# Fused attention and channel mix on one core: block 2 fetches its input tiles once for two mixes, and the parts of the kernel stand in a newly planned order

## The chip, the cores and the metric

The kernel runs on one core of a Trainium2 chip. The metric is the device time of one execution in microseconds (us), lower is better. The engines of the core are named as in the profile: PE (matmuls; PEld is its weight load), DVE (vector), ACT (scalar), POOL, and SP, whose queue issues nearly all DMA transfers.

## What is computed

An attention in two steps gives x, and a channel mix works on x. Sizes: 8 batches, 8 heads, 576 positions, head dimension 64, 32 pack keys; x has 8 x 576 = 4608 rows of 512; all inputs are fp32.

```
def attention(q, k, v, p):                  # per batch and head
    packed = softmax(p @ k.T / 8) @ v       # 32 x 64
    return softmax(q @ packed.T / 8) @ packed   # 576 x 64

x = heads side by side                      # (8, 576, 512)
x_prev = x one position later (zeros ahead of the first)
xk = mu_k * x + (1 - mu_k) * x_prev
xr = mu_r * x + (1 - mu_r) * x_prev
k = max(xk @ w_k, 0)                        # 512 -> 1024
v = (k * k) @ w_v                           # 1024 -> 512
out = sigmoid(xr @ w_r) * v
```

## The kernel before

**Blocks.** The 4608 rows of x are nine blocks of 512 rows (TB). Blocks 0, 1 and 2 are computed one by one: first `gates` (xr by w_r, 16 groups of matmuls), then `keys` (xk by w_k, 32 groups), then `values` (the squares by w_v, 32 groups). Blocks 3 and 4, 5 and 6, 7 and 8 are three pairs (PAIRS), in which products of sums of blocks and sums of weights are taken (`products_of`, L1499); the first pair's gates are `turned_gates` (L1655 to L1657, 32 groups). A product is split for precision: each operand is a high and a low part, and high by high, high by low and low by high are added. So a group is three matmuls of 128x128 by 512 columns, called a triple here (L1087 to L1089 and L1109 to L1111 in the gates, L1038 to L1040 in the keys, L1138 to L1140 in the values).

**Attention.** It runs batch by batch, its small matmuls set between the triples: `front` (L630, the pack queries by the 4 key tiles kT of a batch, 32 matmuls), L658 (the weights by v), L688 (a transpose), L786 (q by the packed keys; when it is done, the places of that batch's key and query tiles are free for a later batch's), and two groups of L835 (16 matmuls each), which make x of a batch. Batch 0, the first gates and the conversion of the weights into high and low parts (`convert`, L351 to L367) form the head of the program; where PE would have nothing to do there, it runs spare matmuls (L1833). The mixes of block 0 are made from PSUM in the head (`mixed_on_pe`: L892 on PE, L903 on ACT, L905 on DVE).

**The input of a block.** Blocks 0 and 1 (`FETCHED = 2`) take x from SBUF. From batch 1 on x is also stored in DRAM (the tiles xt into xd, 577 KB a store, one for two of the four 128-channel slices), and blocks from 2 on read it back. `mix(i, j, res, tag)` makes the four slices c of one mix of block i, one after another: it starts `fetch(i, c, j)`, waits for it, takes places, mixes (`mixed_parts`: L1006 on ACT times mu, then L1010 on DVE, which adds the shifted x) and starts `split` (L1019 on ACT: high part; L1021 on DVE: low part). It stands for xr and for xk of a block, so a slice is fetched twice. The places "xin" at block 2 are two.

**What sets the order.** Every part of the work is a generator with a rank. The class `Flow` holds the time at which each engine would be free by estimated durations, and at each step emits the instruction that could start first, the lower rank first where starts are equal. So the order of the instructions on PE, DVE, ACT and in SP's queue follows from the estimates and from a table of ranks at the top of the kernel; each engine then runs its own instructions strictly in that order on the chip, and SP issues its transfers in that order too, each when what it waits for has come. `load` (L247) is the estimate for a transfer: it takes one shared DMA resource for `us`, times 1.3 between 1.2 and 8 us, and `1.1 * us + 0.1` where it begins after 45 us.

**Squares.** `squared` takes a finished key group: ACT relu (L1050), ACT square (L1053), then the high part: on ACT (L1058) for the first `CASTS = 2` of the eight f of a block, on DVE (L1061) for the others; then the low part on DVE (L1063).

**Sums of weights.** For the pairs, DVE and ACT make sums of the split weights in spare time (`chain_of_sums`, tiles sw), which SP stores in DRAM (sum<-sw) and streams back later (ring<-sum).

Of the kernel before, what the change touches and what calls it, by code (L numbers as in the profile page):

```python
# [17 lines left out]
class Flow:  # L18
# [12 lines left out]
    HOLD = {}  # L31
    URGENT = 22.872
    CHANGE = 0.1
# [157 lines left out]
def attn_pack_channel_mix(ctx: ExitStack, tc: tile.TileContext, q, k, v, p, p_first, mu_first, mu_by_channel, w_k, w_v, w_r, out):  # L191
    nc = tc.nc
    B, NPR, P, S = q.shape
# [17 lines left out]
    flow = Flow()  # L211


    FIRST = 14.499, 7.547, 12.422, 11.979
    RANK_1, RANK_MIX, RANK_KEYS, RANK_R, RANK_W, RANK_W2, RANK_V, LOADS_1, RANK_SQ, RANK_REST, HOLD_V, HOLD_S = 12.717, 12.505, 15.753, 30, 30, 27.28, 30, 30, 0.73, -9.153, 0.319, 0.199
    RANK_LATE1 = -1.745
    RANK_LATE2 = 1.396
    RANK_LATE3 = 8.576
    RANK_LATE4 = 9.62
    RANK_LATE5 = 9.05  # L220
    RANK_LATE6 = 13.793
    RANK_LATE13 = 8.231
    RANK_LATE12 = -0.408
    FIRST_K, FIRST_V, FIRST_Q = (RANK_LATE1, RANK_LATE2), (RANK_LATE3, RANK_LATE4), (RANK_LATE5, RANK_LATE6)
# [20 lines left out]
    def load(dst, src, issue, us, queue="queue"):  # L245
        yield queue, issue, None, None
        dict(queue=nc.sync, scalar=nc.scalar, gpsimd=nc.gpsimd)[queue].dma_start(dst, src)  # L247
        begin = max(flow.free.get("dma", 0.0), flow.t + 0.46, SLOW[0])
        if begin < SLOW[1]:
            us *= SLOW[2]  # L250
        elif begin > 45.0:
            us = 1.1 * us + 0.1
        flow.free["dma"] = begin + us
        flow.free[queue] = max(flow.free[queue], begin - 2.0)
        flow.now.t = begin + us + LANDS

    LANDS = 2.0
# [5 lines left out]
    def reached():  # L263
# [12 lines left out]
    BUFS = dict(kq=7, vt=2, xin=0, pt=1, aT=4, pm=2, e=4, a2=1, xt=5, tmp=4, xk=NC, sq=NF, sig=4,  # L276
                pa=2, both=1, m=4, n=4, staged=4, ex=3, pair=0, ring=0, store=2, twin=0)
    for tag, n in BUFS.items():
# [9 lines left out]
    MORE = {("tmp", 4): "ex2"}  # L288
    RANK_B, RANK_TURN, RANK_BACK, RANK_OUT, RANK_L = 3.794, 1.444, 9.553, 2.981, 27.75
    CASTS = 2  # L290
    WHOLE = dict(wv=0)
    RANK_AHEAD = 9.346
    RANK_2, LOADS_2 = 11.443, 34.522
    RANK_SUMS = dict(k=26.146, v=2.238, r=29.743)
    CHAINS = dict(A=(13.692, 26.413), B=(37.551, 41.281), RB=(0.2, 15.996), C=(16.813, 2.931), RC=(3.842, 6.82))

# [655 lines left out]
    def mix(i, j, res, tag):  # L952

        yield from flow.wait("mu")
        rank = flow.now.rank
        for c in range(NC):
            if i < FETCHED:
                yield from flow.wait(*(("xt", b, c, hf) for b, *_ in pieces(i) for hf in range(2)))
            else:
                flow.spawn(fetch(i, c, j), rank)  # L960
                yield from flow.wait(("fetched", i, c, j))
            slot = yield from flow.take("xk" if tag == "xk" else "sq")
            space = "tmp"
            sx = yield from flow.take(space)
            x32 = tile_([P, TB], F32, space, sx, "x32")
            yield from (mixed if i < FETCHED else mixed_parts)(i, c, j, x32)
            flow.spawn(split(i, c, space, sx, x32, res, tag, slot), rank)
# [15 lines left out]

    fetched = {}

    def fetch(i, c, j):
# [3 lines left out]
        at, parts = 0, []  # L990
        for b, s, n, o in pieces(i):
# [4 lines left out]
            at += n + 1  # L996
        fetched[i, c, j] = slot, parts
        flow.set(("fetched", i, c, j))

    def mixed_parts(i, c, j, x32):  # L1000
# [7 lines left out]
        for n, o, x in parts:  # L1008
# [3 lines left out]
            )  # L1012
        flow.give("xin", slot)

# [734 lines left out]
    def channel_mix():  # L1749
# [16 lines left out]
        for i in PAIRS:  # L1766
# [4 lines left out]
            for t in range(NF // 2):  # L1771
                flow.spawn(operands_of_values(i, t), 1.091)
            for kind in KINDS[i]:
# [133 lines left out]
```

## Time and profile before

| | us |
|---|---|
| three runs | 552.84, 556.06, 553.84 |
| their median | 553.84 |
| the profiled execution, whole | 552.96 |
| its span in the profile | 551.2 |
| PE busy | 540.6 (98%) |
| DVE busy | 463.9 (84%) |
| ACT busy | 379.1 (69%) |

The span is the stretch from the first to the last instruction that the profiler recorded; the 1.8 us between it and the execution's own time lie around it. The profiled execution is 0.88 us below the median of the three runs. The granted clock of PE was 0.999 of full speed over the span.

### The profile page before, as it was taken

To read this page: it belongs to the slowest core of one execution; us is meant where nothing else is said; L and a number is where in the kernel's file an instruction comes from. 1 tells how busy PE (TensorE), PEld (TensorE's weight loads), DVE (VectorE), ACT (ScalarE), POOL (GpSimd) and SP (SyncE) were. 2 spreads that over 40 slices of the span, in tenths; PEclk is the share of its full clock that TensorE was granted. 3 is DMA by queue.
4 is the path that set the end of the run, shared out by engine and by line. 5 is a ranking of instruction groups with operands and counts; after the bars stand their busy time and mean duration, and the time that the engine had idled before them with its cause. 6 is when DMAs were issued, how large, how long until landed. Compare 5 with 4: busy or idle time off the path is not lost.

```text
span 551.2 us, 10089 instructions
## 1 busy us (share of the span) xinstructions
PE 540.6 (98%) x3541; PEld 416.6 (76%) x3541; DVE 463.9 (84%) x887; ACT 379.1 (69%) x730; POOL 2.8 (1%) x27
## 2 busy tenths in 40 slices
PE   8999999999999999999999999999999999999996
PEld 7857766766677777776887888887878888888885
DVE  2987989987799958898898999957999994799873
ACT  3789686556746756648899666589886648987650
POOL 1000000000000000000000000000000000000000
PEclk9999999999999999999999999999999999999999
DMA  8977967798977889697938537819273680924232
GB/s 301 401 282 242 398 225 262 234 296 266 298 245 238 273 284 347 194 319 237 318 135 278 199 134 226 252 50 294 78 229 95 219 259 28 303 92 153 76 134 96
DMA packets 90386, 123.89 MB, mean 225 GB/s; under 512 B 9824, under 2 KB 60512, under 8 KB 90336
## 3 DMA queue, kind: packets, MB, share of 16 engines
q1 hardware_dynamic: 89056, 121.87, 67.5%
q10 hardware_dynamic: 1280, 1.38, 0.7%
q8 instruction: 28, 0.46, 0.3%
q14 instruction: 22, 0.18, 0.1%
HBM read 89.38 MB, written 33.83 MB: 224 GB/s over the span
## 4 chain that ended last, share of the span: by engine, by line
PE 70%; DMA 14%; DVE 7%; ACT 5%; issue 2%; SPq 1%; POOL 0%; DVEq 0%; ACTq 0%; POOLq 0%
PE ph L1499 48%; DMA xin<-xd 3%; PE ph L1038 3%; PE ph L1039 2%; PE ph L1040 2%; DMA sum<-sw 2%; PE spare L1833 2%; DMA kT<-in_k 2%; DMA whole<-m 1%; PE pr L1656 1%; PE pr L1657 1%; PE pr L1655 1%; SPq L247 1%; PE pa L630 1%; DVE x L1010 1%
## 5 line engine op out<-in xcount | busy, mean ns | idle before, releaser
L1499 PE MATMUL ph<-vT,ring 128*128 128x512 f32 x270 | 66.5, 393 | 0.0
L1499 PEld LDWEIGHTS ph<-vT,ring 128*128 128x128 f32 x270 | 50.7, 188 | 11.5
L1499 PE MATMUL ph<-vB,wv_h 128*128 128x512 f32 x140 | 43.9, 395 | 0.1
L1499 PE MATMUL ph<-vT,wv_h 128*128 128x512 f32 x140 | 43.7, 394 | 0.0
L1138 PE MATMUL pvo<-wv_h,sq 128*128 128x512 f32 x96 | 39.5, 412 | 0.5 <-ACT r L1050 0.5
L1038 PE MATMUL ph<-xk,wk_h 128*128 128x512 f32 x96 | 39.2, 408 | 0.0
L1010 DVE SCALAR_TENSOR_TENSOR chain<-xin,mus,chain 128x320 f32<-128x320 f32 (+7 forms) x72 | 34.5, 509 | 5.1 <-ACT chain L1006 5.0
L1139 PE MATMUL pvo<-wv_l,sq 128*128 128x512 f32 x96 | 37.6, 391 | 0.0
L1039 PE MATMUL ph<-xk,wk_h 128*128 128x512 f32 x96 | 37.5, 391 | 0.0
L1040 PE MATMUL ph<-xk,wk_l 128*128 128x512 f32 x96 | 37.4, 390 | 0.0
L1140 PE MATMUL pvo<-wv_h,sq 128*128 128x512 f32 x96 | 37.4, 389 | 0.0
L1551 ACT COPY ph<-ph 128x512 f32<-128x512 f32 x44 | 25.4, 577 | 15.3 <-PE ph L1499 14.9
L1006 ACT ACTIVATE chain<-xin,mus 128x320 f32<-128x320 f32 (+7 forms) x72 | 35.3, 525 | 0.0
L1157 ACT CAST vT<-c 128x512 fp32r<-128x512 f32 x40 | 24.7, 619 | 14.7 <-PE ph L1499 12.8
L1163 DVE TENSOR_TENSOR c<-c 128x512 f32<-128x512 f32 x48 | 31.0, 685 | 0.0
L1499 PEld LDWEIGHTS ph<-vB,wv_h 128*128 128x128 f32 x140 | 26.1, 188 | 6.4 <-DMA wv_h<-sum 0.7
L1499 PEld LDWEIGHTS ph<-vT,wv_h 128*128 128x128 f32 x140 | 26.2, 188 | 6.0 <-ACT ph L1551 0.3
L1159 DVE TENSOR_TENSOR vT<-c,vT 128x512 fp32r<-128x512 f32 x40 | 26.7, 687 | 2.4 <-ACT vT L1157 2.3
L1499 PE MATMUL ph<-vB,wv_l 128*128 128x512 f32 x70 | 27.6, 395 | 0.3 <-DMA wv_l<-sum 0.3
L1499 PE MATMUL ph<-vT,wv_l 128*128 128x512 f32 x70 | 27.4, 391 | 0.0
L1163 DVE TENSOR_TENSOR chain<-chain 128x512 f32<-128x512 f32 x40 | 26.7, 685 | 0.3
L1159 DVE TENSOR_TENSOR vT<-chain,vT 128x512 fp32r<-128x512 f32 x32 | 21.4, 686 | 5.5 <-ACT vT L1157 5.3
(206 smaller groups left out, 1374.3 us busy)
## 6 DMA issues: line engine op xcount, KB each, us to landing
ring<-sum SPq DMA_DIRECT2D x56, 256.0 KB, 4.1
sum<-sw SPq DMA_DIRECT2D x40, 256.0 KB, 4.1
kT<-in_k SPq DMA_DIRECT2D x32, 288.0 KB, 5.5
qT<-in_q SPq DMA_DIRECT2D x32, 288.0 KB, 5.4
vt<-in_v SPq DMA_DIRECT2D x32, 256.0 KB, 4.7
out<-sig SPq DMA_DIRECT2D x32, 256.0 KB, 3.3
xd<-xt SPq DMA_DIRECT2D x14, 577.0 KB, 6.3
wv_h<-sum SPq DMA_DIRECT2D x28, 256.0 KB, 4.2
```

Source lines behind the costliest of these rows:

```text
L1006: nc.scalar.mul(x32[:, o:o + n], x[:, 1:], mus[:, j, c:c + 1])
L1010: nc.vector.scalar_tensor_tensor(x32[:, o:o + n], x[:, :n], mus[:, j + 1, c:c + 1], x32[:, o:o + n], op0=ALU.mult, op1=ALU.add,)
L1038: nc.tensor.matmul(ph, wk_h[:, c, fs], xh, start=(c == 0), stop=False)
L1039: nc.tensor.matmul(ph, wk_h[:, c, fs], xl, start=False, stop=False)
L1040: nc.tensor.matmul(ph, wk_l[:, c, fs], xh, start=False, stop=(c == NC - 1))
L1138: nc.tensor.matmul(pv[t], sh, wv_h[:, f, :], start=(n == 0), stop=False)
L1139: nc.tensor.matmul(pv[t], sh, wv_l[:, f, :], start=False, stop=False)
L1140: nc.tensor.matmul(pv[t], sl, wv_h[:, f, :], start=False, stop=(n == NF - 1))
L1159: nc.vector.tensor_tensor(lo, x32, hi.bitcast(F32), op=ALU.subtract)
L1163: nc.vector.tensor_tensor(out, x, y, op=op)
L1499: nc.tensor.matmul(bank[2], w, x, start=(not more and step == k == 0), stop=(step == 2 and k == count - 1), skip_group_check=True,)
L1551: nc.scalar.copy(bank[2], base)
```

## The change

**1. One fetch for both mixes of block 2.** For a block that is fetched and stands before the pairs (only block 2), the mix "xk" no longer starts a fetch. It waits for the fetch that "xr" has made (j = 2) and takes the same tile; `users` counts the two, and the second of them gives the place back. Of the 16 transfers xin<-xd of block 2 eight are gone.

**2. Casts.** `CASTS` goes from 2 to 6: of the 24 casts of the squares of blocks 0 to 2, twelve move from DVE (L1061) to ACT (L1058).

**3. The planner's estimate of a transfer.** `1.1 * us + 0.1` holds from 8 us on, not only after 45 us, and a load on ACT's queue that begins before 10 us is taken to land 1 us later. This puts out no instruction; it moves the planned order.

**4. Places and ranks.** There are three places, not two, for sums that wait to be stored (`store`), and nearly all ranks have new values. What is computed and the number of instructions stay the same but for points 1 and 2 and for one spare matmul more.

```diff
-    URGENT = 22.872
+    URGENT = 25
...
-    FIRST = 14.499, 7.547, 12.422, 11.979
+    FIRST = 20.716, 6.677, 25, 24.059
...
         if begin < SLOW[1]:
             us *= SLOW[2]
-        elif begin > 45.0:
+        else:
             us = 1.1 * us + 0.1
         flow.free["dma"] = begin + us
         flow.free[queue] = max(flow.free[queue], begin - 2.0)
-        flow.now.t = begin + us + LANDS
+        flow.now.t = begin + us + LANDS + (1.0 if queue == "scalar" and begin < 10.0 else 0.0)
...
-                pa=2, both=1, m=4, n=4, staged=4, ex=3, pair=0, ring=0, store=2, twin=0)
+                pa=2, both=1, m=4, n=4, staged=4, ex=3, pair=0, ring=0, store=3, twin=0)
...
-    CASTS = 2
+    CASTS = 6
...
-    RANK_SUMS = dict(k=26.146, v=2.238, r=29.743)
+    RANK_SUMS = dict(k=32.85, v=20.602, r=23.848)
...
             if i < FETCHED:
                 yield from flow.wait(*(("xt", b, c, hf) for b, *_ in pieces(i) for hf in range(2)))
+            elif i < PAIRS[0] and tag == "xk":
+                yield from flow.wait(("fetched", i, c, 2))
+                fetched[i, c, 0] = fetched[i, c, 1]
+                flow.set(("fetched", i, c, 0))
             else:
                 flow.spawn(fetch(i, c, j), rank)
                 yield from flow.wait(("fetched", i, c, j))
...
-    fetched = {}
+    fetched, users = {}, {}
...
-        fetched[i, c, j] = slot, parts
+        fetched[i, c, j] = fetched[i, c, 1] = slot, parts
+        if i < PAIRS[0]:
+            users[i, c] = 2
         flow.set(("fetched", i, c, j))
...
-        flow.give("xin", slot)
+        if i < PAIRS[0]:
+            users[i, c] -= 1
+        if i >= PAIRS[0] or not users[i, c]:
+            flow.give("xin", slot)
```

Lines from L1010 on stand 9 lines further down in the changed kernel (L1087 is L1096 there), L977 is L981.

**On PE, at the end of the head.** The first gates (pr, L1087 to L1089), the two sums of shifted tiles L921, and the front of batch 1 (L630) stand like this before, from the first L921 on; five gate triples are ahead of the front, counted from the start of the gates:

```order
L921 MATMUL pa_570<-a2t_191,pm_303 128x65 x2
L921 MATMUL pa_570<-a2t_191,pm_368 128x65 x2
L1087 MATMUL pr_540<-wr_h_130,xr_473 128x512
L1088 MATMUL pr_540<-wr_l_131,xr_473 128x512
L1089 MATMUL pr_540<-wr_h_130,xr_473 128x512
L1087 MATMUL pr_583<-wr_h_130,xr_458 128x512
L1088 MATMUL pr_583<-wr_l_131,xr_458 128x512
L1089 MATMUL pr_583<-wr_h_130,xr_458 128x512
L630 MATMUL pa_596<-kT_227,pt_178 32x288
```

The same place of the changed kernel:

```order
L1096 MATMUL pr_568<-wr_h_130,xr_458 128x512
L1097 MATMUL pr_568<-wr_l_131,xr_458 128x512
L1098 MATMUL pr_568<-wr_h_130,xr_458 128x512
L921 MATMUL pa_580<-a2t_191,pm_300 128x65 x2
L921 MATMUL pa_580<-a2t_191,pm_360 128x65 x2
L1096 MATMUL pr_568<-wr_h_130,xr_482 128x512
L1097 MATMUL pr_568<-wr_l_131,xr_482 128x512
L1098 MATMUL pr_568<-wr_h_130,xr_482 128x512
L1096 MATMUL pr_481<-wr_h_130,xr_503 128x512
L1097 MATMUL pr_481<-wr_l_131,xr_503 128x512
L1098 MATMUL pr_481<-wr_h_130,xr_503 128x512
L630 MATMUL pa_602<-kT_227,pt_178 32x288
```

Seven gate triples stand ahead of the front now, two more than before.

**On DVE, at the last xr slice of block 1.** L977 adds the shifted x into x32, L1021 makes the low part of xr from it, L1149 multiplies finished values of block 0 with the gate. Before:

```order
L977 SCALAR_TENSOR_TENSOR x32_1416<-xt_1053,mus_122,x32_1416 128x448
L705 TENSOR_REDUCE mx_1515<-pa_1495 128x1
L1149 TENSOR_TENSOR sig_660<-pvo_1123,sig_660 128x512
L1149 TENSOR_TENSOR sig_700<-pvo_1131,sig_700 128x512
L1149 TENSOR_TENSOR sig_720<-pvo_1150,sig_720 128x512
L1021 TENSOR_TENSOR xr_1536<-x32_1416,xr_1536 128x512
L707 TENSOR_SCALAR nmx_1516<-mx_1515 128x1
```

The same place of the changed kernel:

```order
L981 SCALAR_TENSOR_TENSOR x32_1422<-xt_1055,mus_122,x32_1422 128x448
L676 TENSOR_SCALAR rs_1483<-sm_1106 128x2
L818 TENSOR_SCALAR m2_1367<-m2_1367 128x18
L678 RECIPROCAL rs_1483<-rs_1483 128x2
L820 RECIPROCAL m2_1367<-m2_1367 128x18
L801 STREAM_TRANSPOSE e_1317<-pa_1295 128x576
L1030 TENSOR_TENSOR xr_1441<-x32_1422,xr_1441 128x512
L682 TENSOR_TENSOR pm_1487<-pa_1378,rs_1483 128x128
L1158 TENSOR_TENSOR sig_637<-pvo_1077,sig_637 128x512
```

The low part of xr stood behind three multiplications of block 0's values; it stands ahead of the first of them now.

**In SP's queue, at the first fetch of block 2.** xd_136 and xd_137 are the DRAM copies of batch 2's x, xd_138 and xd_139 those of batch 3; kT are key tiles, sum a stored sum of weights, xin the fetched input. Before:

```order
L247 DMA xd_138<-xt_1960 128x1154
L247 DMA xd_139<-xt_1962 128x1154
L247 DMA aT_1932<-away_1933 32x4x160 x2
L247 DMA sum_154<-sw_2001 128x512
L247 DMA kT_2067<-in_k 128x576
L247 DMA xin_2095<-xd_134 128x129
L247 DMA xin_2095<-xd_136 128x385
L247 DMA xin_2096<-xd_134 128x129
L247 DMA xin_2096<-xd_136 128x385
```

The same place of the changed kernel:

```order
L247 DMA xd_137<-xt_1619 128x1154
L247 DMA sum_149<-sw_1936 128x512
L247 DMA xin_2062<-xd_134 128x129
L247 DMA xin_2062<-xd_136 128x385
L247 DMA sum_152<-sw_1804 128x512
L247 DMA sum_150<-sw_2027 128x512
L247 DMA xd_138<-xt_2022 128x1154
L247 DMA xd_139<-xt_2024 128x1154
L247 DMA sum_153<-sw_2053 128x512
L247 DMA kT_2171<-in_k 128x576
```

Before, the stores of batch 2's x (xd_136, xd_137) stand 24 and 25 rows ahead of the first fetch, with batch 3's between. In the changed kernel the store of xd_137 stands two rows ahead of it, and xd_136 nine; behind the fetch come batch 3's stores and kT_2171, the fourth key tile of batch 6.

Along PE, the front of batch 5 comes 14 triples behind the L786 group that frees the place of its fourth key tile (11 before), that of batch 6 nine (14 before), and that of batch 7 eleven and one L835 group (26 before). Batch 7's fourth key tile stands in SP's queue behind the second of block 1's four output stores. The last L835 group stands behind three triples of the turned gates, not behind eleven.

## Rows read from the trace of the kernel before

**Rows 1.** The page's first part: busy time, share of the span, instructions of each engine.

```profile
PE 540.6 (98%) x3541; PEld 416.6 (76%) x3541; DVE 463.9 (84%) x887; ACT 379.1 (69%) x730; POOL 2.8 (1%) x27
```

**Rows 2.** By stretch: length, busy PE, PEld, DVE, ACT, POOL (instructions), clock, DMA, GB/s.

```profile
0.00:41.60 41.60, 38.87 (x315) 29.29 (x315) 27.68 (x54) 26.14 (x52) 1.57 (x15) 1.00 0.89 327
41.60:273.70 232.10, 229.07 (x2051) 167.59 (x2052) 201.88 (x430) 154.82 (x303) 1.22 (x12) 1.00 0.84 275
273.70:547.00 273.30, 272.70 (x1177) 219.70 (x1175) 233.55 (x403) 198.09 (x376) 0.00 (x0) 1.00 0.53 169
```

**Rows 3.** PE's waits: line, releaser, us in total, times, longest.

```profile
PE pa L630 <- DVE xk L905: 1.1, 1, 1.1
PE pa L630 <- DMA kT<-in_k: 1.1, 2, 0.9
PE pr L1655 <- ACT xr L1019: 0.7, 1, 0.7
PE pr L1111 <- DVE nmx L707: 0.4, 1, 0.4
PE pr L1656 <- DVE xr L1021: 0.2, 1, 0.2
```

**Rows 4.** PE at the end of the head: start, length, instruction, idle before and releaser.

```profile
41.62 1.36 PE L630 MATMUL pa<-kT,pt 64*32 64x288 f32 x32 [1.14 <-DVE xk L905]
42.91 0.50 PE L1087 MATMUL pr<-wr_h,xr 128*128 128x512 f32 x1
```

**Rows 5.** PE at the fronts of two batches that wait for a key tile.

```profile
130.93 0.70 PE L630 MATMUL pa<-kT,pt 64*32 64x288 f32 x12
132.51 1.16 PE L630 MATMUL pa<-kT,pt 64*32 64x288 f32 x20 [0.88 <-DMA kT<-in_k]
133.60 0.50 PE L1038 MATMUL ph<-xk,wk_h 128*128 128x512 f32 x1
...
197.75 0.70 PE L630 MATMUL pa<-kT,pt 64*32 64x288 f32 x12
198.65 1.16 PE L630 MATMUL pa<-kT,pt 64*32 64x288 f32 x20 [0.20 <-DMA kT<-in_k]
199.74 0.50 PE L1038 MATMUL ph<-xk,wk_h 128*128 128x512 f32 x1
```

**Rows 6.** PE: end of block 0's values, L786 that frees key places, an L835 group.

```profile
109.60 0.39 PE L1140 MATMUL pvo<-wv_h,sq 128*128 128x512 f32 x1
...
121.20 1.20 PE L786 MATMUL pa<-qT,ppT 64*32 64x288 f32 x32
...
124.60 0.74 PE L835 MATMUL pa<-a,pm 32*64 32x288 f32 x16
```

**Rows 7.** SP's queue between 111 and 138 us: output stores, a key tile, two x stores.

```profile
111.04 1.53 SPq L247 DMA_DIRECT2D out<-sig  x3
...
127.24 0.37 SPq L247 DMA_DIRECT2D kT<-in_k  x1
...
128.95 0.84 SPq L247 DMA_DIRECT2D xd<-xt  x2
...
131.09 2.50 SPq L247 DMA_DIRECT2D qT<-in_q  x2
136.88 0.33 SPq L247 DMA_DIRECT2D away<-blocks  x1
```

**Rows 8.** DMA issues of key tiles: instructions, KB each, median us to landing.

```profile
kT<-in_k SPq DMA_DIRECT2D x32, 288.0 KB, 5.5
```

**Rows 9.** Groups by form: the casts on DVE and ACT; busy us, mean ns, idle before.

```profile
L1061 DVE CAST sq<-r 128x512 fp32r<-128x512 f32 x18 | 7.6, 420 | 4.5 <-ACT r L1053 3.6 <-PE pvo L1140 0.4 <-ACT sw L1318 0.3
L1058 ACT CAST sq<-r 128x512 fp32r<-128x512 f32 x6 | 3.7, 617 | 0.1
```

**Rows 10.** Block 2: its first fetch (SP's queue), its fourth gate triple (PE).

```profile
153.54 1.76 SPq L247 DMA_DIRECT2D xin<-xd  x3
...
184.19 0.39 PE L1109 MATMUL pr<-wr_h,xr 128*128 128x512 f32 x1
```

More of the change, by code (lines that the diff above doesn't have):

```diff
@@ L211, in attn_pack_channel_mix @@
     flow = Flow()
-    FIRST = 14.499, 7.547, 12.422, 11.979
[L215 to L221, printed above, removed]
+    FIRST = 20.716, 6.677, 25, 24.059
+    RANK_1, RANK_MIX, RANK_KEYS, RANK_R, RANK_W, RANK_W2, RANK_V, LOADS_1, RANK_SQ, RANK_REST, HOLD_V, HOLD_S = 11.383, 10.044, 19.844, 26.75, 29.95, 9.922, 30, 30, 0.161, 3.163, 0.153, 0.297
+    RANK_LATE1 = -2
+    RANK_LATE2 = 0.186
+    RANK_LATE3 = 0.833
+    RANK_LATE4 = 6.675
+    RANK_LATE5 = 0.983
+    RANK_LATE6 = 9.737
     RANK_LATE13 = 8.231
-    RANK_LATE12 = -0.408
+    RANK_LATE12 = 12.724
     FIRST_K, FIRST_V, FIRST_Q = (RANK_LATE1, RANK_LATE2), (RANK_LATE3, RANK_LATE4), (RANK_LATE5, RANK_LATE6)
@@ L288, in attn_pack_channel_mix @@
     MORE = {("tmp", 4): "ex2"}
-    RANK_B, RANK_TURN, RANK_BACK, RANK_OUT, RANK_L = 3.794, 1.444, 9.553, 2.981, 27.75
-    CASTS = 2
+    RANK_B, RANK_TURN, RANK_BACK, RANK_OUT, RANK_L = 0.463, 1.444, 9.972, 4.485, 12.537
+    CASTS = 6
     WHOLE = dict(wv=0)
-    RANK_AHEAD = 9.346
-    RANK_2, LOADS_2 = 11.443, 34.522
-    RANK_SUMS = dict(k=26.146, v=2.238, r=29.743)
-    CHAINS = dict(A=(13.692, 26.413), B=(37.551, 41.281), RB=(0.2, 15.996), C=(16.813, 2.931), RC=(3.842, 6.82))
+    RANK_AHEAD = 3.014
+    RANK_2, LOADS_2 = 21.207, 37.339
+    RANK_SUMS = dict(k=32.85, v=20.602, r=23.848)
+    CHAINS = dict(A=(42.11, 3.007), B=(15.264, 2.957), RB=(0.2, 0.2), C=(42.16, 0.715), RC=(0.375, 3.317))
     def banks(slot):
@@ L1771, in channel_mix @@
             for t in range(NF // 2):
-                flow.spawn(operands_of_values(i, t), 1.091)
+                flow.spawn(operands_of_values(i, t), 0.807)
             for kind in KINDS[i]:
```

## Prediction

> **What bounds the kernel now.** I began with the page's busy times: PE is busy for 98% of the span, DVE for 84%, ACT for 69% [rows 1]. PE is the bound, so time can only come from PE's waits, from its spare matmuls in the head, or from a matmul taking longer. The matmuls themselves stay the same. The cut by stretch then says where there is anything to win [rows 2]. The head ends at 41.6 us. From 273.7 to 547.0 us PE has 1177 matmuls in 273.3 us, 0.232 us each and without holes: nothing to win there, only to lose, should the sums come late. So the change can act on the head and on the 232 us of the single blocks, where DVE is busy for 201.9 of 232.1 us (87%) and ACT for 154.8 (67%). The granted clock is 1.00 in all three stretches, the higher of its two levels (2.4 GHz), and PE has no long idle time, so I expect no change there.
>
> The list of PE's waits names what can be won [rows 3]: 1.1 us at the end of the head (front L630 for DVE's L905), 1.1 us for key tiles, 0.7 and 0.2 us at the turned gates for xr, 0.4 us in the gates of block 1. The view understates each wait: a matmul of 512 columns is drawn 0.39 us long, while they follow each other at 0.23, so each wait costs 0.16 us more than is listed. The key tiles cost more still. The front of 32 matmuls takes 1.29 us where it runs through (41.62 to 42.91) [rows 4]; split after its twelfth by a late key tile it took 130.93 to 133.60 and 197.75 to 199.74, which is 2.67 and 1.99 [rows 5], 1.38 + 0.70 = 2.08 us lost.
>
> **The head: -1.1.** Two more gate triples (six matmuls, 6 x 0.23 = 1.38 us) stand ahead of the front in the changed order, in place of 1.14 us of idle time [rows 4]. The front waits for the eviction L905, whose place in the work is the same; if that ends when it does now, the idle time is filled and PE is ahead by 1.14 us. I subtract 1.1. Bounds: -1.3 if the drawn end hides 0.16 more; 0 if the evictions of the head come as much later as the triples come earlier, since DVE's and ACT's conversions are in a new order there and I can't price that from the trace.
>
> **Last xr of block 1: -0.55.** In the gates of block 1 PE waits 0.4 us (+0.16) for DVE [rows 3]. In the old order the low part of xr stands behind three multiplications of values; now it stands ahead of them. I counted DVE's and PE's instructions ahead of this one in both orders, from the last eviction of the head on, each with the mean length of its group in the profile (an estimate): 56.4 us of work instead of 64.3 lie ahead of it, against 54.5 instead of 55.9 on PE: 6.5 us more room than now. Bounds: 0 to -0.55.
>
> **Turned gates: -1.2.** The same count gives 3.9 us more room for the last xr slice of block 4 (180.0 against 185.3 us of work ahead on DVE, PE about 1.4 less), more than the two waits of 0.7 + 0.2, with 2 x 0.16 [rows 3]. Bounds: 0 to -1.2.
>
> **Key tiles: -2.08, then +1.6.** A fourth key tile can be fetched when an L786 group has freed its place. For batch 5 that group ends at 122.40 [rows 6], but SP issues the tile at 127.24 [rows 7]: 4.84 us late, since the queue runs in order and stands at other transfers. From issue to landing such a tile takes 5.5 us [rows 8]. In the new order batch 5 has 14 triples between (11 before), so it should not wait; the two waits of now go (-2.08). New ones can come:
> - Batch 6 has nine triples and a transpose, about 9 x 0.69 + 0.3 = 6.5 us. The tile stands behind the stores of batch 3's x. An x store was issued 3.6 us after the L835 group that completes it (125.34 to 128.95) [rows 6, 7], and from that group to the end of the L786 group are three triples, an L658 group and L786 itself (1.20, and L658 taken as the same), 4.5 us, so SP should come to the tile at about the time it is free: 0 to 0.5 + 5.5 against 6.5. I take +0.3; bounds 0, and 4.84 + 5.5 - 6.5 = 3.8 if it is as late as in batch 5.
> - Batch 7's tile stands behind the second of block 1's output stores. After block 0's values, which end at about 109.83 [rows 6], three such stores were issued from 111.04 in 1.53 us [rows 7], so two until 112.06, or 2.2 us behind the last matmul; 5.5 us later the tile lands, 7.7 us behind it. PE comes to the front after eight triples and an L835 group, 8 x 0.69 + 0.74 + 0.1 = 6.4 us. I take the difference, +1.3; bounds 0 and 2.6 (twice that, as the stores may wait for DVE).
>
> The Trainium skill, "DMA: Bandwidth & Descriptors", section "Anatomy of one DMA — SWDGE (gpsimd) path", fits a transfer as about 2.0 us plus its bytes at 436 GB/s, for transfers issued by GpSimd. An estimate from that page is 2.7 us for a key tile; then neither wait would come, the sum would be -4.3 and the time 549.0. The trace has twice that length for SP's tiles [rows 8], so the sum goes by the trace.
>
> **Casts: 0.** DVE loses 12 x 0.420 = 5.0 us and ACT gains 12 x 0.617 = 7.4 us [rows 9], DVE being busy for 87%, ACT for 67% [rows 2]. What hides the 7.4 us is ACT's idle third. Where ACT is late, the next relu is late and then the first values triple; that would show as a wait of L1138. The cast itself is 0.2 us longer on ACT but two hops between engines go. Bounds: -0.5 to +1.5 (two casts more ahead of a relu that PE waits for).
>
> **Sharing the fetch: 0.** Eight transfers go, with eight issues on SP of at most 0.59 us (three in 1.76 us) [rows 10]. PE is never stopped by block 2's tiles now, so this frees room and no time. But the tile is held longer: its place comes back when both mixes have read it. With two places, the third slice's fetch waits until xk of the first is mixed. xk stands just behind xr in rank, so the price is about one mix on DVE, and I leave it at 0; bound +1.
>
> **Estimate of transfers, places, ranks.** They issue nothing; their effect is the order counted above. New orders bring waits that no count shows: I add +0.6, one wait of the middle size in the list.
>
> **Sum.** -1.1 - 0.55 - 1.2 - 2.08 + 1.6 + 0.6 = -2.7. Against the profiled execution's 552.96 that is 550.2. It lies 0.88 us below the median of the three runs and 0.12 above the lowest; I add half of the distance, 0.4: **550.6 us**.
>
> **The rivals.**
> - *The waits only move.* The head's gain is eaten by later evictions, and batches 6 and 7 wait at the upper bounds' middle. Then -0.55 - 1.2 - 2.08 + 3.2 + 0.6 = 0, or with the +0.4 a time of **553.3**. For it: PE is at 98%, and SP's queue was 4.84 us late at such a tile. Against it: both xr waits have several us more room.
> - *Nothing new waits.* The head gives 1.3, the key tiles land in time, no unseen wait: -1.3 - 0.55 - 1.2 - 2.08 = -5.1, **548.2**.
> - *Slower: SP's queue holds block 2's first fetch.* From the issue of the first fetch to the fourth gate triple of block 2 are 30.65 us now (153.54 to 184.19) [rows 10], four rounds of fetch, mix and split one after another. PE doesn't wait there, so the chain takes no more. In the new order the fetch stands behind the store of batch 2's second x and behind a sum made by DVE in spare time. From the end of the L835 group that completes this x to the fourth gate triple are 46 triples and the small groups between, 46 x 0.69 + 9 = 40.6 us: the fetch may start some 10 us behind that group. The old x store was issued after 3.6 us; so it takes 6.4 us more of waiting in the queue, for the sum or the places, until PE is late by this. The widest hole of the queue here is 3.3 us (133.59 to 136.88) [rows 7], the late key tile 4.84; both together are 8.1, and PE would be 1.7 us late, and as late again in the xk of block 2, as the tiles are shared: +3.4, **554.0**. It ends above the time of before (553.84) once the queue has waited 8.0 us, and above the bound for slower from 9.4 us on. The Trainium skill, "DMA: Bandwidth & Descriptors", section "Rules for kernel authors", says that a transfer which reads what another wrote in DRAM has to wait for its completion before it is issued; by that a late store holds all of the queue behind the fetch too. No row here shows such a stop.
> - *The change does nothing* (sharing and casts are off the path and the order is as good as the old): 553.3 too; it is one with the first rival.
>
> **How the numbers follow.** The forecast has 0.45 (549 to 552.4), the moved waits 0.28, nothing new 0.10, the slower case 0.17. What a measurement of this kernel can tell from no change is about 0.5%, 2.77 us: faster is below 551.07, slower above 556.6. Faster: two thirds of the first case, all of the third, a little of the second: 0.44. Slower: most of the last case's longer delays, 0.13. Same: 0.43. The range leaves out 0.1 on each side: 547.4, a little under the third case, to 555.6, in the last.
>
> **What would show it.** In the changed profile: no wait of L630 for L905 near 41 us, or one under 0.4; no wait of the gates of block 1 and of the turned gates for xr; waits of L630 for kT in the second half of the single blocks, in sum 1 to 2 us; L1061 with 6 casts, L1058 with 18; eight fetches xin<-xd fewer; from 273.7 on 0.232 us a matmul. It would be wrong if a wait for xr or xk of block 2 of over 1 us shows (the slower case), if values wait for a relu, or if the pairs wait for sums.

## The result, and the profile after

The changed kernel takes 557.34 us (median of seven runs, 555.03 to 558.44), the kernel before 552.84 in runs beside it (551.67 to 556.06). The ratio is 1.0072, with an interval of 1.0046 to 1.0099: some 4 us slower, where 3 us faster was forecast. The profiled execution took 557.94, its span 556.0, the granted clock over the span was 0.994.

The page's first part, to read beside [rows 1]:

```profile
PE 543.6 (98%) x3543; PEld 418.2 (75%) x3543; DVE 456.6 (82%) x875; ACT 387.3 (70%) x742; POOL 2.8 (1%) x27
```

DVE has 7 us less to do, ACT 8 more; most of this, 4.5 and 6.7 us, goes with the casts (with the casts back, below, DVE has 461.1 and ACT 380.6). Of the 4.8 us by which the span grew, 3.0 are busy time of PE and 1.8 its idle time. What PE waits for, to read beside [rows 3]:

```profile
PE pa L835 <- DVE a L827: 2.4, 1, 2.4
PE pvo L1147 <- ACT r L1059: 2.0, 1, 2.0
PE spare L1842 <- POOL ident masks.py:199: 1.5, 1, 1.5
PE ph L1508 <- DMA wv_h<-sum: 1.0, 2, 0.5
PE pr L1120 <- DVE xr L1030: 0.6, 1, 0.6
PE pa L688 <- DVE pm L682: 0.4, 1, 0.4
PE pa L835 <- DVE blocks L752: 0.3, 1, 0.3
```

The kernel before has one wait that [rows 3] leaves out, at the values of block 0:

```profile
PE pvo L1138 <- ACT r L1050: 0.5, 1, 0.5
```

All the waits that the change was to remove are gone, and there is none for a key tile. Two long ones have come, longer than any of [rows 3]: 2.0 us at the first values of block 1, 2.4 us at the turned gates. Where they lie, by the first matmul of each stage in the two traces (attention stands between the stages, in other places in the two orders, so only the first and the last columns compare nearly the same work):

| first matmul, us | keys(1) | values(1) | gates(2) | values(2) | turned gates | pairs |
|---|---|---|---|---|---|---|
| before | 123.83 | 154.23 | 182.14 | 221.84 | 248.55 | 273.59 |
| changed | 122.34 | 150.45 | 182.58 | 225.68 | 251.59 | 278.37 |

The changed kernel is 1.5 us ahead at keys(1) and 4.8 us behind at the pairs. The pairs are alike: from their first matmul to the start of the last 273.0 us before, 273.5 after. So the loss lies between 150 and 262 us. The two waits and what follows them, in order of time (start, length, instruction, idle before and releaser):

```profile
156.35 0.60 ACT L1059 ACTIVATE r<-ph 128x512 f32<-128x512 f32 x1 [3.16 <-DMA sum<-sw]
157.01 0.53 PE L1147 MATMUL pvo<-wv_h,sq 128*128 128x512 f32 x1 [2.04 <-ACT r L1059]
157.34 0.62 PE L1148 MATMUL pvo<-wv_l,sq 128*128 128x512 f32 x1
157.76 0.63 PE L1149 MATMUL pvo<-wv_h,sq 128*128 128x512 f32 x1
158.32 2.17 PE L786 MATMUL pa<-qT,ppT 64*32 64x288 f32 x32
...
255.31 0.77 DVE L827 STREAM_TRANSPOSE a<-e 128x576 f32<-128x576 f32 x1
256.23 1.25 PE L835 MATMUL pa<-a,pm 32*64 32x288 f32 x16 [2.44 <-DVE a L827]
...
258.43 0.63 PE L1666 MATMUL pr<-xr,wr_l 128*128 128x512 f32 x1
258.86 0.63 PE L1664 MATMUL pr<-xr,wr_h 128*128 128x512 f32 x1
259.28 0.61 PE L1665 MATMUL pr<-xr,wr_h 128*128 128x512 f32 x1
```

The first wait goes back to a DMA. The relu of the last key group needs a place of "tmp"; three of these five may now hold sums that wait to be stored (`store=3`), and the relu got the place of one whose store was issued at 150.51 behind another of 577 KB and landed at 156.33. After each wait matmuls stand 0.42 us apart instead of 0.23, and an L786 takes 2.17 instead of 1.20 [rows 6]: in this execution each wait is followed by some 1.6 us of slower matmuls. By stretch (columns as in [rows 2]), the changed kernel:

```profile
150.00:159.00 9.00, 6.96 (x127) 4.22 (x133) 1.80 (x7) 4.01 (x10) 0.10 (x1) 0.91 1.00 373
159.00:186.00 27.00, 27.00 (x208) 19.10 (x187) 27.00 (x56) 15.09 (x33) 0.20 (x2) 0.97 0.77 230
208.00:222.00 14.00, 14.00 (x161) 10.14 (x160) 5.67 (x13) 10.28 (x21) 0.20 (x2) 1.00 0.91 312
222.00:256.00 34.00, 31.79 (x229) 22.75 (x227) 32.93 (x68) 20.07 (x42) 0.20 (x2) 1.00 0.73 232
156.50:162.00 5.50, 4.99 (x41) 2.66 (x42) 3.51 (x8) 4.01 (x9) 0.20 (x2) 0.69 0.79 289
254.00:262.00 8.00, 5.77 (x31) 4.06 (x32) 6.90 (x17) 4.74 (x12) 0.00 (x0) 0.79 0.90 316
```

and the kernel before, in the first four of these stretches:

```profile
150.00:159.00 9.00, 9.00 (x67) 6.53 (x65) 8.04 (x16) 3.89 (x7) 0.20 (x2) 1.00 0.96 328
159.00:186.00 27.00, 27.00 (x270) 19.70 (x270) 26.54 (x59) 17.42 (x38) 0.00 (x0) 1.00 0.72 211
208.00:222.00 14.00, 14.00 (x101) 10.29 (x100) 13.07 (x28) 8.10 (x17) 0.20 (x2) 1.00 0.97 335
222.00:256.00 34.00, 33.05 (x281) 23.89 (x280) 31.33 (x68) 22.32 (x46) 0.10 (x1) 1.00 0.83 265
```

The third busy figure, DVE's, is the one to look at. DVE works 1.80 of 9 us where it had worked 8.04, and 5.67 of 14 where it had worked 13.07. In the stretches behind these it is full, 27.00 of 27 and 32.93 of 34, but there it was nearly full before too, 26.54 and 31.33. So what is new are the two holes of DVE, 7.2 and 8.3 us. The longest idle times in them (the last brackets: length and releaser) are

```profile
155.07 0.29 DVE L682 TENSOR_TENSOR pm<-pa,rs 128x128 f32<-128x128 f32 x1 [4.00 <-PE pa L658]
158.49 0.43 DVE L1070 CAST sq<-r 128x512 fp32r<-128x512 f32 x1 [3.13 <-PE pvo L1149]
213.00 0.69 DVE L1072 TENSOR_TENSOR sq<-r,sq 128x512 fp32r<-128x512 f32 x1 [2.10 <-ACT sq L1067]
216.25 0.69 DVE L1072 TENSOR_TENSOR sq<-r,sq 128x512 fp32r<-128x512 f32 x1 [2.56 <-ACT sq L1067]
```

In the first hole DVE waits for a group of the attention on PE, then for the PE that the relu has stopped; in the second it waits twice for a cast on ACT (L1067). The chain that ended last names DVE too. Its shares by engine, the changed kernel's:

```profile
PE 77%; DVE 11%; DMA 6%; ACT 3%; issue 2%; SPq 1%; POOL 0%; DVEq 0%; ACTq 0%; POOLq 0%
```

and of before:

```profile
PE 70%; DMA 14%; DVE 7%; ACT 5%; issue 2%; SPq 1%; POOL 0%; DVEq 0%; ACTq 0%; POOLq 0%
```

In the changed kernel's chain the long pieces between 159.77 and 185.45 us and between 223.50 and 256.23 are DVE's but for one; its last ones (start, length, engine, tile, line) are

```profile
183.87 1.58 DVE x L1016 x4
185.45 0.69 DVE a L827
...
250.68 2.40 DVE sig L1158 x4
253.85 0.75 DVE e L822
255.39 0.70 DVE a L827
256.23 1.25 PE pa L835 x16
```

No wait of PE stands between 159 and 182 us, so the list of PE's waits alone would not have shown the first of these stretches.

### The profile page after: what moved, and what is told of

Its sections match the earlier page's. It is cut to its first block, busy times and chain, and to the rows that moved or that the text cites. A ratio compares the mean times of both kernels' runs of the same rounds, so it can differ in the third digit from the quotient of the medians.

```text
span 556.0 us, 10088 instructions
## 1 busy us (share of the span) xinstructions
PE 543.6 (98%) x3543; PEld 418.2 (75%) x3543; DVE 456.6 (82%) x875; ACT 387.3 (70%) x742; POOL 2.8 (1%) x27
## 3 DMA queue, kind: packets, MB, share of 16 engines
q10 hardware_dynamic: 1280, 1.38, 0.7%
## 4 chain that ended last, share of the span: by engine, by line
PE 77%; DVE 11%; DMA 6%; ACT 3%; issue 2%; SPq 1%; POOL 0%; DVEq 0%; ACTq 0%; POOLq 0%
PE ph L1508 47%; PE ph L1047 3%; PE spare L1842 3%; PE ph L1048 2%; PE ph L1049 2%; DMA sum<-sw 2%; DVE x L1016 2%; DMA wv_h<-sum 2%; PE pvo L1147 1%; PE pa L892 1%; PE pr L1664 1%; PE pr L1665 1%; PE pvo L1149 1%; PE pvo L1148 1%; PE pr L1666 1%
## 5 line engine op out<-in xcount | busy, mean ns | idle before, releaser
L1149 PE MATMUL pvo<-wv_h,sq 128*128 128x512 f32 x96 | 37.6, 392 | 0.0
L1147 PEld LDWEIGHTS pvo<-wv_h,sq 128*128 128x128 f32 x96 | 18.1, 188 | 11.9 <-issue 5.4
```

What stands on the lines that cost most here:

```text
L1147: nc.tensor.matmul(pv[t], sh, wv_h[:, f, :], start=(n == 0), stop=False)
L1149: nc.tensor.matmul(pv[t], sl, wv_h[:, f, :], start=False, stop=(n == NF - 1))
```

## The experiments

Where a kernel holds an order, each engine's instructions stand in it one for one, and only the edit shown differs. Ratios are to the kernel before, run beside it.

**The relu's place.** The changed order; the relu of block 1's last key group and the sum made ahead of it exchange their places of "tmp".

```diff
-next sum: place B            | relu: place A, its store still queued
+next sum: place A            | relu: place B, free
```

> The changed kernel, every engine in the same order; only two of the five places 'tmp' are swapped, so that the last relu of block 1's keys writes where a finished square lay and not where a sum of weights waits for its store to land; the next sum takes that place. Theory A (with three sums allowed to wait, one holds the relu's place until its store, issued late in SP's queue, has landed; PE then waits 2.0 us and runs at the lower clock for some 4 us): PE's wait of L1147 for ACT falls from 2.0 to under 0.3 us, the granted clock between 156.5 and 162 us is 1.00 and not 0.69, and the time falls by 2.0 + 0.16 + some 1.6 = 3.8, from 557.3 to about 553.5. Rival B (ACT has twelve more casts and is late by itself): the wait stays between 1.5 and 2.0 us, time 557. Rival C (DVE is the bound behind it): the wait goes, but the wait of L835 at the turned gates, 2.4 us now, grows by as much, time 556 to 557.

556.9 us, ratio 1.0065 (1.0037 to 1.0092). The wait for the relu is gone and the clock stays at 1.00 until 162 us, values(1) to gates(2) takes 28.6 us instead of 32.1. Then PE waits longer at block 2's gates, 0.9 and 0.7 us where it had waited 0.6:

```profile
PE pa L835 <- DVE a L827: 2.5, 1, 2.5
...
PE pr L1118 <- ACT xr L1028: 0.9, 1, 0.9
PE pr L1120 <- DVE xr L1030: 0.7, 1, 0.7
```

```profile
182.00:188.00 6.00, 4.95 (x14) 3.64 (x15) 6.00 (x12) 2.48 (x5) 0.00 (x0) 0.72 1.03 302
```

The last xr of block 2 is split at 183.1 us here, at 183.5 before, at 186.1 in the changed kernel. So the wait at 157 us was real, and taking it away only let PE run into the next limit: a wait is not a sum that comes back.

**Casts.** Back to 2 in the changed order, and to 6 in the order of before.

```diff
-    CASTS = 6        # changed kernel
+    CASTS = 2
...
-    CASTS = 2        # kernel before
+    CASTS = 6
```

> The changed kernel with CASTS = 2 again, in the same order of parts: the twelve casts go back from ACT to DVE, each at its place. Theory A: the casts have no part in the wait at block 1's values, L1147 waits 2.0 us again; DVE has 5 us more work ahead of the turned gates, where PE already waits 2.4 us for it, so that wait grows by some of it: 557 to 561. Rival B (the casts on ACT make the relu late): the wait of L1147 falls under 0.5 us, time 553 to 555.

> The kernel before with CASTS = 6 alone, in its own order: twelve casts go from DVE to ACT. The prediction's term: 0 (bounds -0.5 to +1.5), 552.3 to 554.3. If DVE's lateness at the turned gates (waits of 0.7 and 0.2 us for xr) is due to its load, they shrink, up to -1.2. Rival B (ACT becomes late): a wait of L1138 for the relu of 1 us or more, time 554 or more.

557.36 us, ratio 1.0086 (1.0053 to 1.0119), and 554.07, ratio 1.0022 (0.9995 to 1.005). Both new waits are there in the first, 2.24 and 2.44 us in the profiled execution (560.22), yet no matmul behind them is slow and the clock stays at 1.00:

```profile
158.06 0.50 PE L1147 MATMUL pvo<-wv_h,sq 128*128 128x512 f32 x1 [2.24 <-ACT r L1059]
158.96 1.20 PE L786 MATMUL pa<-qT,ppT 64*32 64x288 f32 x32
```

```profile
156.50:162.00 5.50, 3.94 (x43) 2.56 (x44) 2.87 (x7) 4.16 (x9) 0.20 (x2) 1.00 0.86 335
254.00:262.00 8.00, 5.56 (x38) 4.05 (x37) 6.90 (x18) 5.15 (x12) 0.00 (x0) 1.00 0.86 298
```

The casts cost nothing that can be told; they are not the cause. And the same wait at the same place is followed by the lower clock in one execution and not in another.

**Sharing alone**, in the order of before: the eight fetches for xk left out, the tile held for both mixes.

```diff
+        again = i < PAIRS[0] and j == 0
...
+            if again:
+                yield "queue", 0.46, None, None
+                continue
```

> The kernel before with block 2's tiles fetched once, in its own order: the eight fetches of xk are left out and xk reads xr's tile, the slices in the two places by turns. The prediction's term: 0, 552.8 within 1 us. Rival: eight issues fewer in SP's queue let the key tile behind them come earlier, the second wait for a key tile (0.70 us lost at 198) goes, time 552.1. Rival on the other side: xk now reads late from a tile that the fetch two slices later needs, a wait of the gates or keys of block 2 of 0.5 us or more, time 553.5 or more.

552.89 us, ratio 0.9986 (0.9957 to 1.0015). Sharing costs nothing, and brings nothing that can be told. What is left is the order, with the places that its steps take.

**Four of its moves, put into the kernel before**: those on which the forecast counted.

```diff
-front of batch 1 | two gate triples
+two gate triples | front of batch 1
-front of batch 5 (7) | four (two) triples
+four (two) triples | front of batch 5 (7)
-three multiplications of values | last xr of block 1
+last xr of block 1 | three multiplications of values
```

> The kernel before, all of its code and ranks, with four instructions groups moved in its order and nothing else: the front of batch 1 stands two gate triples later, the front of batch 5 four triples later, that of batch 7 two later, and the low part of block 1's last xr slice ahead of the three multiplications of block 0's values. If the prediction's terms were sized rightly (head -1.1, key tiles -1.4 and -0.7, xr of block 1 -0.55), the time falls by up to 3.7, from 553.4 to about 549.7, and PE's list shows no wait of L630 for a key tile and for L905 over 0.4 us, none of L1111. Rival A (what is gained ahead is lost at the next bound: DVE and the fetches aren't earlier, so PE comes earlier to the turned gates and waits there for xr by as much more): waits of L1655 and L1656 grow from 0.9 to 2 us and more, time 552 to 553. Rival B: the moved fronts come too late for DVE, time 553 or more.

555.65 us, ratio 1.0014 (0.9992 to 1.0036). The waits for L905, for key tiles and for block 1's xr are gone, 2.6 us of [rows 3], and nothing is gained: block 2's xr comes at the same times as before (162.8 to 183.4 us), and the waits for relus and for copies of ACT grow from 0.5 to 3.4 us in sum.

**Ranks and code apart**, each planned anew: the new code with the old table, the old code with the new table.

```diff
-    URGENT = 25           # and all ranks of the table
+    URGENT = 22.872
...
-    URGENT = 22.872       # the other way about
+    URGENT = 25
```

> The changed kernel with the ranks of before (URGENT, FIRST, all RANK_ values and CHAINS); the shared fetch, CASTS = 6, the estimate of transfers and the third place for sums stay. The order is planned anew from these. Theory (the ranks that put the attention of batches 2 to 6 later make the loss, and not the code): the last L835 group of batch 2 and the L786 group of batch 6 stand as far ahead as in the kernel before, no wait of 2 us at the turned gates, 551 to 555. Rival (the code's parts, or the estimate with the third place, make it): 556 or more.

> The kernel before with the new ranks alone; no shared fetch, CASTS = 2, the old estimate and two places for sums. Theory (the new ranks make the loss): attention late again, waits at the turned gates of 2 us or more, 556 or more. Rival (the new ranks only fit the new code or are harmless): 551 to 555.

565.11 us, ratio 1.0184 (1.0157 to 1.0211), and 569.3, ratio 1.0262 (1.0234 to 1.0291). Each table fits its own code; neither half alone carries the loss of 4 us.

**A late relu in the kernel before**: the last relu of block 0's keys made four times, same values.

```diff
-        nc.scalar.activation(r, ph, AF.Relu)
+        [nc.scalar.activation(r, ph, AF.Relu) for _ in range(4 if (i, f) == (0, 7) else 1)]
```

> The kernel before, its order; the relu that PE waits for at the start of block 0's values (L1050, 0.60 us on ACT) is done four times in a row, which gives the same values, so that PE waits some 1.8 us longer there, 2.3 us. If a wait of this length lowers the granted clock, as at the two places of the changed kernel, the matmuls behind it are spaced by 0.42 us and not by 0.23 for some 3 to 4 us, and the time rises by 1.8 + some 1.6, to 556.5 or more; if not, by 1.8 at most, 555, or less where later waits take it up.

557.04 us, ratio 1.006 (1.0028 to 1.0091): 1.8 us more for ACT cost 3.3. PE waits 2.4 us and then runs at the lower clock:

```profile
83.00:86.00 3.00, 0.59 (x3) 0.48 (x3) 1.16 (x3) 2.87 (x6) 0.00 (x0) 1.00 0.54 195
86.00:89.00 3.00, 3.00 (x9) 2.28 (x8) 2.34 (x5) 0.80 (x3) 0.00 (x0) 0.53 0.05 12
```

In the profiled execution (555.22 us, 1.8 below the median) gates(1) start 4.0 us later, the pairs 2.1: about half of the delay is made up on the way.

**The places of delay moved, one by one**, in the changed order: batch 6 of the attention 5.5 us earlier; block 2's fetches a slice ahead, with the relu's place; both.

```diff
-keys(2) triples | L786 of batch 6 | L786 of batch 7
+L786 of batch 6 | keys(2) triples | L786 of batch 7
...
-                flow.spawn(fetch(i, c, j), rank)
+                for n in range(c and c + 1, min(c + 2, NC)) if i < PAIRS[0] else (c,): flow.spawn(fetch(i, n, j), rank)
```

> The order of the changed kernel is held; only the scores, the softmax and the turning back of batch 6 of the attention stand about 5.5 us earlier, ahead of batch 7's scores. Theory: the stretch from 222 to 256 us, in which VectorE has no hole, is a jam that the late batches make; it loosens, the matmul of line 835 waits under 1 us at the turned gates instead of 2.4, the granted clock there stays at 1.00 instead of 0.79, and the kernel takes about 554 us (3 to 4 less than the changed kernel). Rival: VectorE's amount of work sets the end of that stretch, whatever its order; the wait stays at 2 us or more, or TensorE loses the same elsewhere, and the time stays near 557.

> The two places of e1_places_swapped, and block 2's four shared fetches issued one slice ahead of the place that they had in SP's order, with the mixes and splits of its slices 2 to 4 moved forward by 3, 4 and 5 us of planned time. Theory: what took the place of the wait that e1 removed is the chain fetch, mix, split of block 2; with it ahead, the waits of block 2's gates for xr (0.9 and 0.7 us in e1, at a clock of 0.66) go, and the time falls to about 554 us. Rival: the time moves on to the next bound, the wait for VectorE at the turned gates grows beyond 2.5 us, and the kernel stays at 556 to 557.

> Both of the edits of k3_chain and k1_batch6_earlier. Theory: the relu's wait for a store, the fetch chain of block 2 and VectorE's jam ahead of the turned gates are the three places where the changed kernel loses its lead; with all three gone it ends at 550 to 551 us, below both kernels. Rival: the lead is lost to VectorE's amount of work between 41 and 277 us, and no order of these parts brings more than 2 us: 555 or above.

559.61 us, ratio 1.0095 (1.006 to 1.013); 559.05, 1.0099 (1.0068 to 1.0131); 560.86, 1.0128 (1.0094 to 1.0161). All three miss: by the ratios 1 to 3 us slower than the changed kernel, the first two within the noise. In the third the granted clock is 1.00 over the whole span, behind a wait of 2.54 us at the turned gates too, and yet it is the slowest, so the clock is not the whole cost. Its DVE in the last stretch:

```profile
250.00:262.00 12.00, 8.46 (x61) 5.50 (x60) 12.00 (x27) 6.67 (x15) 0.00 (x0) 1.00 0.67 217
```

DVE has no idle time there, wherever these steps stand.

**The attention's places exchanged** as a whole: the changed order's in the kernel before, and the old ones in the changed kernel.

```diff
-attention, order of before  | block stages, order of before
+attention, changed order    | block stages, order of before
...
-attention, changed order    | block stages, changed order
+attention, order of before  | block stages, changed order
```

> The kernel before, in its own order, with one thing changed: the attention's steps (scores, softmax, turning back, the parts that follow) stand where the changed order has them, counted in matmul triples of the blocks; that is 4 to 25 triples later for batches 2 to 6 and up to 16 earlier for batch 7. Theory: these places are what the changed order loses by; VectorE gets holes of 5 us or more in 150 to 160 or 210 to 220 us that the kernel before doesn't have, and the kernel takes 556 to 558 us. Rival: the loss comes from the rest of the order (block stages, fetches, stores); then this stays within 1 us of 553.8.

> The changed kernel, with the attention's steps alone put back to where the order of before has them, counted in triples. Theory: the 4 to 5 us come back and, as the head, block 1's last xr and the key tiles still gain what they gained, it ends at 552 to 554 us. Rival: the rest of the order sets the time; it stays at 556 to 558 us, with waits at the same stages.

585.6 us, ratio 1.0589 (1.0545 to 1.0633), and 585.39, ratio 1.0577 (1.0546 to 1.0607). Both take 31 us more than the kernel before, with many waits of 1 to 5.5 us for DVE and ACT. This tells nothing of the 4 us: the two halves of an order can't be exchanged. Whether these places alone cause DVE's holes stays open.

**DVE relieved.** The additions of block 2's mixes and of the turned gates' xr left out, so that the output is another: 32 instructions, 15.2 us, half in each of DVE's full stretches (DVE's busy time falls by 11.3 us in the changed order); in the changed order, in the order of before, and in the changed order with the relu's place.

```diff
-            nc.vector.scalar_tensor_tensor(
+            if engine: engine.scalar_tensor_tensor(
```

> The changed kernel in its own order, with VectorE's 32 additions of line 1016 left out that make block 2's mixes and the turned gates' xr (x keeps only its first product, so the output is another); 16 of them, 7.8 us, stand at 159 to 186 us and 16, 7.6 us, at 231 to 258. Theory: VectorE is the bound there; the wait of 2.4 us for a at the turned gates falls under 1, the granted clock at 254 to 262 us stays at 1.00, and the kernel takes 553 to 555 us (the wait for the store at 157 us stays). Rival: transfers, or the order of the steps, bound both stretches; it stays at 556 to 558.

> The kernel before with the same 32 additions left out (line 1010 there). Theory, by which only the new order has VectorE as its bound: at most 1 us is gained, 552.8 to 554. Rival: VectorE bounds both orders alike; then this gains as much as n1, 2.5 us or more.

> n1 with the two places of e1_places_swapped as well, so that the relu at 156 us waits for no store. Theory: with VectorE relieved, what e1 gained at 157 us is kept (in e1 VectorE's full stretch to 186 us took it back): 3 us below n1, 550 to 552. Rival: it is lost again at block 2's gates, as in e1; within 1 us of n1.

552.59 us, ratio 0.999 (0.9963 to 1.0016); 550.72, 0.9953 (0.9935 to 0.9971); 551.97, 0.9979 (0.9953 to 1.0005). The changed kernel gains 4.7 us, the kernel before 2.3 (553.03 beside it). PE's waits in the first, and its last stretch:

```profile
PE pvo L1147 <- ACT r L1059: 2.0, 1, 2.0
PE spare L1842 <- POOL ident masks.py:199: 1.5, 1, 1.5
PE pa L835 <- DVE a L827: 1.2, 1, 1.2
```

```profile
254.00:262.00 8.00, 8.00 (x37) 6.62 (x36) 5.68 (x15) 6.81 (x13) 0.00 (x0) 1.00 0.97 335
```

In the profiled execution the wait at the turned gates is halved, and the clock stays up there and behind the wait of 2.0 us that has stayed. The first matmul of the pairs stands at 271.77 us (changed order), 271.38 (before) and 271.52 (with the relu's place): in these traces the 4.8 us between the two orders are gone. By the medians only half of the distance is: 0.0037 of the time, 2.0 us, is left of 0.0072, and the profiled execution of the changed order (550.44) lies 2.1 us below its median. The rest goes with the clock. Six of the twelve executions had a granted clock of 0.999 or 1.000 over the span and took 550.27 to 552.09 us; six had 0.993 to 0.997 and took 553.09 to 556.30. All twelve of the order of before had 0.999 or 1.000 and took 549.98 to 551.75; all seven of the changed kernel had 0.990 to 0.997. So with DVE relieved the two orders take the same time where the clock holds. What makes it fall in one execution and not in the next is not shown.

By the theory the kernel before should have gained 1 us at most; that it gains too was the rival's, true for half of the gain, so DVE is near the bound in both orders. By the ratios the two gains are 0.0082 and 0.0047 of the time; their difference, 0.0035 or 1.9 us, is not separated from nothing by intervals of 0.0018 to 0.0027 to each side. So that the new order loses by DVE is likely by the traces, and not shown by the times. The relu's place, from which 3 us were expected here, brings 0.6, less than can be told.

**The same relief with the output kept**: the subtractions of the splits (16 of 0.68 us, 10.9 us in sum) on POOL, in the changed order and in that of before.

```diff
-        nc.vector.tensor_tensor(xl, x32, xh.bitcast(F32), op=ALU.subtract)
+        (nc.vector if i < FETCHED else nc.gpsimd).tensor_tensor(xl, x32, xh.bitcast(F32), op=ALU.subtract)
```

> The changed kernel in its own order, with the 16 subtractions of line 1030 of blocks 2 and up (0.68 us each on VectorE, 5.4 us in each of the two full stretches) made by GpSimd. Theory, VectorE's amount of work in these stretches is the bound: two thirds of what n1 took away are gone, so about 3 of n1's 4.7 us, 554 to 555, if one of them takes less than about 2 us on GpSimd. Rival: each xr comes later by what GpSimd takes longer, and VectorE is slowed while GpSimd works; the time stays at 557 or rises.

> The same in the kernel before (line 1021). By the theory about 1.5 of the 2.3 us that n2 took away, 551.5 to 552.5, below both kernels. Rival, as for p1: 553.5 or above.

557.63 us, ratio 1.0087 (1.0057 to 1.0117), and 557.54, 1.0071 (1.0046 to 1.0097). No gain, and a loss of 4 us in the order of before. The groups on POOL, and DVE beside the first of them (160.09 to 161.43 us):

```profile
L1030 POOL TENSOR_TENSOR xr<-x,xr 128x512 fp32r<-128x512 f32 x12 | 16.0, 1331 | 69.7 <-ACT xr L1028 44.9 <-PE pvo L1149 24.8
L1030 POOL TENSOR_TENSOR xk<-x,xk 128x512 fp32r<-128x512 f32 x4 | 5.9, 1485 | 1.1 <-ACT xk L1028 1.1
```

```profile
159.97 1.87 DVE L1016 SCALAR_TENSOR_TENSOR x<-xin,mus,x 128x128 f32<-128x128 f32 x2
```

Two additions take 1.87 us here, 0.87 at 159.77 in the changed kernel. DVE's busy time fell from 456.6 to 455.7 us, though 10.9 us of work had been taken from it (in the order of before from 463.9 to 464.1): what was moved came back as longer instructions. The Trainium skill, "SBUF — State Buffer", section "Who interferes with whom", says that a VectorE instruction with two inputs in SBUF contends with a GpSimd instruction that reads SBUF. The trace agrees: 1.87 us in place of 0.87. No version faster than both kernels was found with the output kept.

## Why the prediction was wrong

- **The head, -1.1: right.** The wait for L905 is gone; the front starts at 41.84 us behind two more triples (1.38 us), against 41.62 [rows 4].
- **Last xr of block 1, -0.55, and the key tiles' -2.08: right as waits.** Both are gone. **The key tiles' +1.6: wrong**, batches 6 and 7 wait for no tile.
- **Turned gates, -1.2: wrong in kind.** The waits for xr [rows 3] are gone, but DVE's work was counted ahead of the xr alone. The stage also holds L835 of batch 7, and its a comes 2.44 us late from the same DVE.
- **Casts 0 and sharing 0: right**, each shown alone.
- **"I expect no change there", of the clock: wrong.** In the profiled execution it was 0.69 from 156.5 to 162 us and 0.79 from 254 to 262; over the span it was 0.990 to 0.997 in all seven executions.
- **The step that failed: "Estimate of transfers, places, ranks ... I add +0.6, one wait of the middle size in the list."** Two waits came, 2.0 and 2.4 us, in the profiled execution each with some 1.6 us of slower matmuls: about 7.6 us, where the term has 0.6. The kernel gave back more than it had gained. A place whose sum waits to be stored holds the relu up, as the exchange of two places shows; that the third sum, which was to issue nothing, makes it so is not shown by itself. The new order leaves DVE idle for 7.2 us of 150 to 159 and 8.3 of 208 to 222. With 7.6 for 0.6 and nothing for the key tiles' +1.6 the sum is +2.7, against 4.8 in the span; the other 2.1 us are not assigned to single steps.
- **The sum itself.** PE's waits were added as if each came back in full. The four moves show that they don't: 2.6 us of waits taken away, nothing gained; nor did the 2.0 us at the relu come back with its place exchanged. DVE, at 87% in the single blocks [rows 2], is a second bound just behind PE: with less to do on it both orders gain.
- **The rivals.** "The waits only move" was the nearest in kind; it lacked the price of the clock. That values would wait for a relu was named as a sign of being wrong, and it came, but not from the casts, to which it was put. "SP's queue holds block 2's first fetch" was right that a queued transfer would hurt and wrong on which: a store of sums stopped a relu, before any fetch.

Shown: the two waits and their releasers, the clock behind them, that casts and sharing are not the cause, so that by elimination the order is, and that less work on DVE in the two stretches speeds up both orders. Likely, and not shown: that DVE's work decides between the orders. Open: which entries of the table make DVE's holes, and why the clock falls behind a wait in one execution and not in another.

## What to carry to other kernels

Where two engines are near their bound, count the second one's work stretch by stretch, in the new order, ahead of each result that the first one waits for: here two holes in the second engine stood ahead of the stretches in which it was the longest part of the chain. A wait that is seen in a trace is worth its length only if what bounds the next stage has room too; one experiment that takes it away shows that sooner than any sum. Places for data that wait to be stored can stop an engine when they come out of a pool that the critical path draws from: ACT stood for 3.16 us here.

## What the runs showed of the hardware

- Behind a wait of PE of 2.0 to 2.5 us the clock fell to its lower level (1.2 GHz, matmuls 0.42 us apart) in some executions and not in others. It fell behind both waits of the changed kernel and behind the 2.4 us of the late relu. It stayed up behind 2.24 and 2.44 us with the casts back, 2.03 in the relieved kernel and 2.54 in the kernel with all places of delay moved. A wait of 1.6 us brought it down with sharing alone (0.95 from 222 to 256 us), and so did two of 0.9 and 0.7 us close together (0.72 from 182 to 188 us). No fall followed the 1.14 us of [rows 4], nor the 1.2 us at the turned gates of the relieved kernel. So the length of a wait does not tell by itself.
- A subtraction of 128x512 takes 0.68 us on DVE and 1.33 to 1.49 on POOL, and while POOL makes it, a DVE addition with two inputs in SBUF took 1.64 us in place of 0.61.
